# Top-32 attention and two feed-forward layers on one core: the weights' sign by ScalarE, three of eight units masked ahead of exp, blocks of one tile, an order planned with other transfer times

## The chip, the cores and the metric

The kernel runs on one core of a Trainium2 chip. The metric is the device time of one execution in microseconds (us); the kernel before takes 1253.52 us, the median of three runs (1252.94 to 1259.25). TensorE is called PE here, VectorE DVE, ScalarE ACT, GpSimd POOL and SyncE SP; all transfers (DMAs) of this kernel are issued by SP.

## The reference

The computation, cut to what matters:

```python
scores = scale * q @ k.T                       # 4 batches, 8 heads, 576 queries and keys, 64 dimensions
kth = the 32nd largest score of each row
e = exp(scores - max) where scores >= kth, else 0
x = (e / (sum(e) + 1e-9)) @ v                  # then one row of 512 for each of 2304 tokens
h = x @ w1i; x = maximum(0.01 * h, h) @ w1o    # 512 -> 2048 -> 512
h = maximum(x @ w2i, 0); out = (s * h * h + b) @ w2o
```

Inputs and outputs are float32. The kernel keeps accuracy near float32 by splitting every matrix into a high and a low float16 half and adding three of the four products (high by high, high by low, low by high).

## The kernel before

**Tiles, units, blocks.** The 2304 tokens are 18 tiles of 128: for each batch four tiles of 128 queries, and for each two batches one tile that holds the last 64 queries of both ("split"). A unit is a pair of heads of one tile, so a tile has 4 units and there are 72 (0 to 71). For each of the two heads of a unit: PE makes the scores (L768), ACT copies them from PSUM to `s` (L774), DVE finds the top 32 by four rounds of max-of-8 (L786) with three replacements of the found values between them (L795). ACT makes exp of all 576 scores into `em` (L808), with the maximum as bias; DVE multiplies it by the mask score >= 32nd and sums the row (L811). ACT and POOL split `em` into float16 halves (`ehl`, L865 and L869), SP turns them by a transposing DMA (`ahl<-ehl`, L873), PE multiplies by the values (`pv`, L897; 27 matmuls) and DVE scales the product by 1 / sum (L826) into `x` (L904). For the first 7 units (`EB`) PE itself does the turning (L838 to L851).

**The feed-forward layers** take blocks of tiles: ten of one tile, then four of two (`NB`, L930). In a block each layer's first product (L1022) makes 128 x 512 of `h` at a time, with 128 columns a matmul for a block of one tile and 256 for two. For layer 1 ACT makes two relus of it (L1050 scale, L1054 scale times -0.01), POOL subtracts them (L1058); for layer 2 ACT makes one relu and POOL squares it (L1062). ACT and POOL make the halves of that, `g` (L1067, L1070), and PE makes the second product (L1093). Layer 1's weights stay on the chip in `wreg`. Layer 2's halves lie in DRAM (`sc16`) and are streamed anew for every block in pieces of 512 KB (L1001), but for two pieces that stay (`kept`).

**The weights' way in.** Each of the four weight matrices comes in 16 blocks as raw float64 bits (L334, L337), 64 blocks in all. DVE shifts the high word (L343); ACT turns the next 16 bits into a rounded integer in the last place (L348, unsigned 16-bit in and out, every fourth half word); DVE cuts sign and top exponent bit beside it (L353); POOL adds the two (L357). Then come a norm for each four blocks (L367 to L413) and the split into halves, in one of several ways (`WM`): P by PE (L458, L461) and ACT (L466, L469), D by ACT (L445) and DVE (L454), G by DVE (L448), ACT (L443) and POOL (L451).

**What sets the order.** All steps go through a planner (`Plan.order`): a step has an engine, a price in us, what it needs, a key and the ring buffers that it takes and frees. Each engine takes, whenever it is free, the ready step with the lowest key. The result is a fixed order on each engine, and at run time every engine works through its list in order and waits at what isn't ready. A transfer's price in the planner is 0.65 us to its start and a duration that differs by kind (2.016 us for `ahl<-ehl`), and 0.91 to 1.0 us until another engine sees it.

```python
            x = add(SP, 2.016, e_turn, [y for _, y in lo], ke, take=[ta], use=[th], issue=0.65)   # L876
```

## Time and profile before

| what | value |
|---|---|
| time, median of 3 runs | 1253.52 us |
| the profiled execution's own time, by its span | 1250.3 us, 3.2 us under that median |
| busy: PE, DVE, ACT, POOL | 1070.3, 1036.9, 827.4, 842.1 us |
| first and last `x` of a unit (L904) | 51.4 and 1098.3 us |
| DMA | 228.39 MB, mean 183 GB/s |

The profile is of one execution. Busy time of an engine is the time in which it has an instruction; a matmul's end is modelled and matmuls overlap, so PE's busy time is above what its matmuls need when they follow each other closely. Idle time of an engine costs only where the engine is the one that all wait for. The page's second part cuts the span into 40 slices of 31 us and gives the busy share of each in tenths.

### The profile page before, as it was taken

How to read it: one execution, taken by the hardware profiler on the slowest of the kernel's cores; microseconds unless marked ns; L12 is line 12 of the kernel's file. 1: busy time of each engine (PE TensorE's matmuls, PEld its weight loads, DVE VectorE, ACT ScalarE, POOL GpSimd, SP SyncE). 2: the span in 40 equal slices, each digit the busy share in tenths (PEclk: the TensorE clock that was granted, in tenths of full speed). 3: DMA queues.
4: the chain of work that ended last, by engine and by line, in shares of the span. 5: the costliest groups of instructions: out<-in, count | busy, mean ns of one | idle time of the engine just before them, and what ended most of it. 6: DMA issues, size and time to landing. Idle time of an engine off the chain costs nothing.

```text
span 1250.3 us, 27997 instructions
## 1 busy us (share of the span) xinstructions
PE 1070.3 (86%) x10520; PEld 735.6 (59%) x10520; DVE 1036.9 (83%) x2437; ACT 827.4 (66%) x1427; POOL 842.1 (67%) x1126
## 2 busy tenths in 40 slices
PE   2666767788888988988998989789989799899998
PEld 1333334556666766665776666566566466666665
DVE  4999899999989999999999999889999999800000
ACT  7887998866577766667876665558876565444321
POOL 5776555657678877677887776658887666655542
PEclk9877898999999999999999999989999999999999
DMA  7767776478889898888899797988445568510444
GB/s 180 237 217 213 198 199 198 148 165 211 218 158 240 199 263 183 220 201 223 221 237 248 165 249 162 261 231 195 83 80 114 149 162 228 153 26 18 133 162 161
DMA packets 362408, 228.39 MB, mean 183 GB/s; under 512 B 276512, under 2 KB 301088, under 8 KB 362272
## 3 DMA queue, kind: packets, MB, share of 16 engines
q1 hardware_dynamic: 362272, 226.61, 71.5%
q8 instruction: 82, 1.34, 0.5%
q14 instruction: 54, 0.44, 0.1%
HBM read 151.52 MB, written 13.11 MB: 132 GB/s over the span
## 4 chain that ended last, share of the span: by engine, by line
DVE 24%; PE 22%; DMA 17%; POOL 9%; issue 4%; ACT 4%; SPq 1%; DVEq 0%; POOLq 0%; ACTq 0%
DMA ahl<-ehl 10%; DVE mx L786 9%; PE acc L1093 9%; PE h L1022 9%; DVE wk L795 8%; DVE em L811 5%; POOL ehl L869 3%; DMA st_o<-sc_2o 2%; PE pv L897 2%; POOL g L1070 2%; DMA qn<-in_q_dram 1%; POOL r L1058 1%; PE sc L768 1%; DMA vn<-in_v_dram 1%; DMA st_i<-sc_2i 1%
## 5 line engine op out<-in xcount | busy, mean ns | idle before, releaser
L786 DVE MAX8 mx<-wk 128x8 f32<-128x576 f32 x432 | 311.3, 744 | 0.0
L1093 PEld LDWEIGHTS <-g 128*128 128x128 f16 x1728 | 159.5, 98 | 141.0 <-issue 23.7
L1022 PE MATMUL h<-early,wreg 128*128 128x128 f16 (+1 forms) x2688 | 224.2, 235 | 5.1 <-DMA early<-xhl 3.5
L1022 PEld LDWEIGHTS <-wreg 128*128 128x128 f16 x2688 | 194.3, 98 | 52.8 <-issue 5.1
L1093 PE MATMUL acc<-wreg,g 128*128 128x512 f16 x864 | 222.8, 380 | 0.2 <-DVE o L1152 0.2
L795 DVE MATCH_REPLACE8 wk<-mx,wk 128x576 f32<-128x576 f32 x288 | 212.7, 741 | 0.0
L1093 PE MATMUL acc<-st_o,g 128*128 128x512 f16 x756 | 194.5, 379 | 12.9 <-DMA st_o<-sc_2o 12.6
L869 POOL TENSOR_TENSOR ehl<-em,ehl 128x576 f16<-128x576 f32 x130 | 168.0, 1298 | 50.1 <-ACT ehl L865 49.7
L1022 PE MATMUL h<-xT,st_i 128*128 128x128 f16 (+1 forms) x2352 | 198.5, 236 | 2.3 <-DMA st_i<-sc_2i 2.0
L1022 PEld LDWEIGHTS <-st_i 128*128 128x128 f16 x2352 | 170.3, 99 | 45.5 <-DMA st_i<-sc_2i 5.0
L1050 ACT ACTIVATE r<-h,cg 128x512 f32<-128x512 f32 x144 | 98.3, 683 | 93.7 <-PE h L1022 74.8
L811 DVE SCALAR_TENSOR_TENSOR em<-s,mx,em 128x576 f32<-128x576 f32 x144 | 155.0, 1087 | 0.3 <-ACT em L808 0.2
L865 ACT CAST ehl<-em 128x576 f16<-128x576 f32 x130 | 86.4, 668 | 93.0 <-DVE em L811 67.1
L808 ACT ACTIVATE em<-s,st,est 128x576 f32<-128x576 f32 x144 | 121.8, 861 | 18.9 <-POOL st L789 14.9
L1067 ACT ACTIVATE g<-r 128x512 f16<-128x512 f32 x144 | 89.9, 626 | 64.1 <-PE acc L1093 44.5
L897 PE MATMUL pv<-vhl,ahl 128*128 128x64 f16 (+3 forms) x2160 | 86.6, 201 | 49.8 <-DMA ahl<-ehl 47.6
L897 PEld LDWEIGHTS <-ahl 128*128 128x128 f16 (+1 forms) x2160 | 79.6, 104 | 71.9 <-DMA ahl<-ehl 66.8
L1058 POOL TENSOR_TENSOR r<-r,early 128x512 f32<-128x512 f32 x72 | 93.6, 1300 | 38.2 <-ACT early L1054 37.9
L1062 POOL TENSOR_TENSOR early<-r 128x512 f32<-128x512 f32 x72 | 75.7, 1052 | 62.1 <-ACT r L1050 61.4
L774 ACT COPY s<-sc 128x576 f32<-128x576 f32 x144 | 91.5, 636 | 35.0 <-PE sc L768 31.8
L768 PE MATMUL sc<-kT,qT 128*128 128x288 f16 (+1 forms) x640 | 99.2, 297 | 11.2 <-ACT s L774 9.7
L786 DVE MAX8 mx<-s 128x8 f32<-128x576 f32 x144 | 107.0, 746 | 0.3 <-ACT s L774 0.3
(191 smaller groups left out, 1741.0 us busy)
## 6 DMA issues: line engine op xcount, KB each, us to landing
st_i<-sc_2i SPq DMA_DIRECT2D x98, 512.0 KB, 4.8
st_o<-sc_2o SPq DMA_DIRECT2D x98, 512.0 KB, 4.8
raw_2i<-in_moe_w_in_dram SPq DMA_DIRECT2D x16, 512.0 KB, 4.9
wreg<-in_moe_w_in_dram SPq DMA_DIRECT2D x16, 512.0 KB, 5.7
raw_1o<-in_moe_w_out_dram SPq DMA_DIRECT2D x16, 512.0 KB, 4.0
raw_2o<-in_moe_w_out_dram SPq DMA_DIRECT2D x16, 512.0 KB, 4.1
qn<-in_q_dram SPq DMA_DIRECT2D x16, 256.0 KB, 4.8
sc_2i<-hl_2i SPq DMA_DIRECT2D x16, 256.0 KB, 2.4
```

The source lines that it names most:

```text
L768: nc.tensor.matmul(pt[a, c, 0:288], lhsT=qT[u][:, h, z, a], rhs=kT[b, p][:, 576 * h + 288 * c:576 * h + 288 * c + 288], start=(z == 0), st ...
L774: nc.scalar.copy(sc[u, h], box["pt"][:, :, 0:288])
L786: nc.vector.max(out=mx[u][:, h, r, :], in_=wk[u, h] if r else flat(sc[u, h]))
L795: nc.vector.match_replace(out=wk[u, h], in_to_replace=mx[u][:, h, r, :], in_values=src, imm_value=NEG)
L808: nc.scalar.activation(em[u][:, h, :], flat(sc[u, h]), AF.Exp, bias=st[u][:, h:h + 1], scale=est[:, 0, u:u + 1])
L811: nc.vector.scalar_tensor_tensor(em[u][:, h, :], flat(sc[u, h]), mx[u][:, h, 3, 7:8], em[u][:, h, :], op0=ALU.is_ge, op1=ALU.mult, accum_o ...
L869: nc.gpsimd.tensor_tensor(ehl[u][:, 1, a], em[u][:, h, :], ehl[u][:, 0, a], op=ALU.subtract)
L897: nc.tensor.matmul(pt[a, o0:o1], lhsT=ahl[u][:, za, blk * P + a.start:blk * P + a.stop], rhs=vt[:, zv, v0:v1], start=(i == 0 and za == 0 a ...
L1022: nc.tensor.matmul(box["h"][:, n * T:(n + 1) * T], lhsT=w[:, ew, c, :], rhs=src[:, ex, c, :], start=(c == 0 and ew == 0 and ex == 0), stop ...
L1050: nc.scalar.activation(box["r1"], box["h"], AF.Relu, scale=cg[:, 2 * l, 3, gi:gi + 1])
L1058: nc.gpsimd.tensor_tensor(box["r1"], box["r1"], box["r2"], op=ALU.subtract)
L1093: nc.tensor.matmul(accs[i, l, tt], lhsT=ghl[i, l, g][:, eg, n * T + tt * P:n * T + (tt + 1) * P], rhs=w[:, ew], start=(f == 0 and eg == 0 ...
```

## The change

What is done differently, by parts:

1. *The weights' way in.* The shift no longer cuts the sign (one operation instead of two, L373). The rest is now written as a 32-bit integer, by ACT in three of four blocks and by DVE in the fourth (`RM`, L380 and L382). ACT then writes the sign, plus or minus 1, as a bfloat16 into the upper half of that word (L386); the integer sum on POOL carries it to the exponent. DVE's cut of the sign goes. The scales get a factor of 2 for it. The norm's 16 matmuls for four blocks are one step (L402), and the ways of making halves differ (`WM`, `A` being ACT, ACT, POOL). The raw blocks' ring `raw` has 2 buffers, not 3, and the order of the matrices is other (`ORDER`).
2. *Masks.* In units 1, 4 and 6 of every 8 (`MK`; 27 of 72 units) ACT makes relu(BIG * (32nd - score)) (L862), POOL subtracts that from the scores (L865), and ACT makes exp of the difference with the row's sum in the same instruction (L868). DVE's mask and sum are left out there.
3. *Layers.* Layer 1's two relus and the difference become one leaky relu on ACT (L1117). Every second square of layer 2 is made by ACT (L1127), the others by POOL (L1129).
4. *Blocks.* One of two tiles, then 16 of one (`BLOCKS`).
5. *Planner.* Each kind of transfer has its issue time, its time to landing and its share of the queue (`XFER`); DVE's and POOL's steps that hold each other up are planned one after the other (`lock`); some rings give their buffers out in program order (`IN_LINE`); all keys are other numbers. `EB` is 11: four more units are turned by PE.

```diff
-        "ahl": 1, ..., "raw": 3, "T": 7, ...
+        "ahl": 1, ..., "raw": 2, "T": 7, ...
-WM = {"1i": "PPP", "1o": "P", "2i": "PG", "2o": "DP"}
-ORDER = ("1i", "1o", "2i", "2o")
+WM = {"1i": "VADV", "1o": "PPPP", "2i": "AGAA", "2o": "DPAP"}
+ORDER = ("1i", "1o", "2o", "2i")
+MK = "DADDADAD"
+RM = "AADA"
-EB = 7
+EB = 11
-NB = 10
+BLOCKS = [2, 1, 1, 1, 1, 1, 1, 1, 1, 1, 1, 1, 1, 1, 1, 1, 1]
-LAG = 0.65
+XFER = {..., "e_turn": (3.3, 5.1, 2.8), "turn": (1.3, 3.3, 1.1), "load": (0.42, 3.8, 1.8), ...}
...
+                    if self.lock[n]:
+                        end = max(now, held["POOL" if e == "DVE" else "DVE"]) + self.dur[n]
+                        held[e] = end
                     if e == "SP":
-                        end = moved = max(now + self.issue[n] + LAG, moved) + self.dur[n]
-                    free[e] = max(now + self.issue[n], end - 1.2) if e == "SP" else end
+                        issue, lat, _ = self.issue[n]
+                        end = moved = max(now + lat, moved + self.dur[n])
+                    free[e] = now + issue if e == "SP" else end
...
-            nc.vector.tensor_scalar(wT[m, f].bitcast(I32), t, 0x07FFFFFF, 3, op0=ALU.bitwise_and, op1=ALU.logical_shift_left)
+            nc.vector.tensor_scalar(wT[m, f].bitcast(I32), t, 3, None, op0=ALU.logical_shift_left)
...
-            nc.scalar.activation(t[:, :, 0], t[:, :, 1], AF.Copy, scale=2.0 ** -13)
+            d = raw[m, f].rearrange("p (n t) -> p n t", t=2)[:, :, 0]
+            if RM[f % len(RM)] == "A":
+                nc.scalar.activation(d, t[:, :, 1], AF.Copy, scale=2.0 ** -13)
+            else:
+                nc.vector.tensor_scalar(d, t[:, :, 1], 2.0 ** -13, None, op0=ALU.mult)
...
-            nc.vector.tensor_scalar(t[:, :, 1], t[:, :, 3], 0xC000, None, op0=ALU.bitwise_and)
+            nc.scalar.activation(raw[m, f].bitcast(BF16).rearrange("p (n t) -> p n t", t=4)[:, :, 1],
+                                 raw[m, f].bitcast(F32).rearrange("p (n t) -> p n t", t=2)[:, :, 1], AF.Sign)
...
+            def t_big(u=u):
+                nc.gpsimd.tensor_tensor(st[u][:, 8:10], mx[u][:, :, 3, 7], big.to_broadcast([P, 2]), op=ALU.mult)
+            def above(u=u, h=h):
+                nc.scalar.activation(em[u][:, h, :], flat(sc[u, h]), AF.Relu, bias=st[u][:, 8 + h:9 + h], scale=-BIG)
+            def less(u=u, h=h):
+                nc.gpsimd.tensor_tensor(em[u][:, h, :], flat(sc[u, h]), em[u][:, h, :], op=ALU.subtract)
+            def expo2(u=u, h=h):
+                nc.scalar.activation(em[u][:, h, :], em[u][:, h, :], AF.Exp, bias=st[u][:, h:h + 1], scale=est[:, 0, u:u + 1],
+                                     accum_out=st[u][:, 2 + h:3 + h])
...
-            x = add(SP, 2.016, e_turn, [y for _, y in lo], ke, take=[ta], use=[th], issue=0.65)
+            x = add(SP, XFER["e_turn"], e_turn, [y for _, y in lo], ke, take=[ta], use=[th])
...
-    for n in [1] * NB + [2] * ((NTL - NB) // 2):
+    for n in BLOCKS:
...
-                nc.scalar.activation(box["r1"], box["h"], AF.Relu, scale=cg[:, 2 * l, 3, gi:gi + 1])
-            def a2(g=g, box=box):
-                nc.scalar.activation(box["r2"], box["h"], AF.Relu, scale=cg[:, 1, 3, g * nf // 4:g * nf // 4 + 1])
-                    nc.gpsimd.tensor_tensor(box["r1"], box["r1"], box["r2"], op=ALU.subtract)
+                    nc.scalar.activation(box["r1"], box["h"], AF.Prelu, scale=cg[:, 0, 3, gi:gi + 1], alpha=0.01)
...
+                if sq == "A":
+                    nc.scalar.activation(box["v"], box["r1"], AF.Square)
+                else:
+                    nc.gpsimd.tensor_tensor(box["v"], box["r1"], box["r1"], op=ALU.mult)
```

Where the instructions stand in the order, at three places. On DVE, while blocks 4 to 6 of matrix 1o come in (`T_1o` is the shifted word, `raw_1o` the raw bits), before:

```order
L343 TENSOR_SCALAR T_1o_4_1333<-raw_1o_4_1253 128x512
L795 MATCH_REPLACE wk_4_0_1283<-mx_4_1263,wk_4_0_1283 128x576
L353 TENSOR_SCALAR raw_1o_4_1253<-raw_1o_4_1253 128x512
L343 TENSOR_SCALAR T_1o_5_1342<-raw_1o_5_1285 128x512
L353 TENSOR_SCALAR raw_1o_5_1285<-raw_1o_5_1285 128x512
L786 MAX mx_4_1263<-wk_4_1_1320 128x8
L343 TENSOR_SCALAR T_1o_6_1352<-raw_1o_6_1307 128x512
```

and now, on ACT, where L380 writes the rest and L386 the sign of block 5 (the other rows are halves of 1i, queries and unit 0's exp):

```order
L756 ACTIVATE qn_1_322<-qn_1_322,cqt_92 128x512
L380 ACTIVATE raw_1o_5_520<-raw_1o_5_520 128x512
L849 ACTIVATE em_0_596<-s_0_0_358,st_0_386,est_93 128x576
L386 ACTIVATE raw_1o_5_520<-raw_1o_5_520 128x512
L771 CAST qhl_4_605<-qn_1_322 128x4x64 x2
```

DVE's L353 is gone from its list; ACT has two instructions for the block where it had one. The same work on 1o stands beside unit 0 now and stood beside unit 4.

On DVE at the end of unit 33, one of the 27 (L811 is the mask, L826 and L892 the reciprocal of the row's sum, `mx_34` the next unit's top 32), before:

```order
L795 MATCH_REPLACE wk_33_1_8325<-mx_33_8248,wk_33_1_8325 128x576
L811 SCALAR_TENSOR_TENSOR em_33_8412,st_33_8249<-s_33_0_8045,mx_33_8248,em_33_8412 128x576
L786 MAX mx_33_8248<-wk_33_1_8325 128x8
L298 TENSOR_SCALAR cvt_84<-vsp_2_1_8439 128x1
L811 SCALAR_TENSOR_TENSOR em_33_8412,st_33_8249<-s_33_1_8078,mx_33_8248,em_33_8412 128x576
L303 TENSOR_SCALAR cvt_84<-cvt_84 128x1
L786 MAX mx_34_8482<-s_34_0_8304 128x8
L795 MATCH_REPLACE wk_34_0_8504<-mx_34_8482,s_34_0_8304 128x576
L298 TENSOR_SCALAR cvt_84<-vsp_2_2_8506 128x1
L826 RECIPROCAL st_33_8249<-st_33_8249 128x2
```

and now, from the last max of unit 33 to its reciprocal:

```order
L827 MAX mx_33_7613<-wk_33_1_7741 128x8
L827 MAX mx_34_7898<-s_34_0_7689 128x8
...
L827 MAX mx_34_7898<-wk_34_0_7916 128x8
L836 MATCH_REPLACE wk_34_1_7969<-mx_34_7898,wk_34_1_7969 128x576
L892 RECIPROCAL st_33_7614<-st_33_7614 128x2
L827 MAX mx_35_8049<-s_35_0_8029 128x8
L1217 SCALAR_TENSOR_TENSOR o_4_8060<-acc_3_1_0_7411,fin_4_6840,bc_85 128x512
```

Both masks are gone. Between the last max and the reciprocal stand 14 instructions now, 13 of them the next unit's search; four stood between the last mask and the reciprocal before.

On PE at the last unit's product (`pv_71`) and what follows it, before:

```order
L897 MATMUL pv_71_16270<-vhl0_94,ahl_71_16233 128x64
L1093 LDWEIGHTS g_12_0_1_16168
L1093 MATMUL acc_12_0_1_16206<-wreg_64,g_12_0_1_16168 128x512
...
L1022 LDWEIGHTS wreg_64
L1022 MATMUL h_12_0_6_16251<-early_63,wreg_64 128x256
```

and now:

```order
L963 LDWEIGHTS ahl_71_17098
L963 MATMUL pv_71_17205<-vhl0_96,ahl_71_17098 128x64
L1088 LDWEIGHTS st_13_i_7_17138
...
L1088 MATMUL h_13_1_3_17170<-xT1_13_16419,st_13_i_7_17138 128x128
L1088 LDWEIGHTS st_13_i_7_17138
```

Behind the last `pv` stood layer 1 of block 12, two tiles; now it is layer 2 of block 13 (tile 14), and the matmuls have 128 columns.

## Rows read from the trace of the kernel before

**Rows 1.** The page: busy time by engine, and two rows of the 40 slices.
```profile
PE 1070.3 (86%) x10520; PEld 735.6 (59%) x10520; DVE 1036.9 (83%) x2437; ACT 827.4 (66%) x1427; POOL 842.1 (67%) x1126
...
PE   2666767788888988988998989789989799899998
DVE  4999899999989999999999999889999999800000
```

**Rows 2.** DVE's timeline: the `x` of unit 11 and that of unit 71 (start, us).
```profile
310.17 0.28 DVE L904 TENSOR_TENSOR x<-pv,st 128x128 f32<-128x128 f32 x1
...
1098.27 0.29 DVE L904 TENSOR_TENSOR x<-pv,st 128x128 f32<-128x128 f32 x1 [8.18 <-PE pv L897]
```

**Rows 3.** Windows by stage: busy us (instructions) of each engine.
```profile
core 0: us, PE busy (x) PEld busy (x) DVE busy (x) ACT busy (x) POOL busy (x), PEclk, DMA share, GB/s
0.00:310.40 310.40, 216.44 (x1660) 130.36 (x1661) 283.06 (x658) 252.89 (x413) 196.30 (x254) 0.91 0.71 195
310.40:787.90 477.50, 429.49 (x5302) 316.40 (x5300) 455.65 (x1086) 330.38 (x594) 359.53 (x512) 0.99 0.89 214
787.90:1098.60 310.70, 277.60 (x2582) 193.39 (x2582) 289.92 (x667) 194.16 (x339) 217.88 (x301) 0.98 0.67 163
1098.60:1250.30 151.70, 146.74 (x980) 95.47 (x977) 8.29 (x30) 50.01 (x85) 68.36 (x60) 1.00 0.32 99
```

**Rows 4.** PE's longest wait from 310 to 1099 us: total, times, longest.
```profile
PE pv L897 <- DMA ahl<-ehl: 44.3, 41, 3.4
```

**Rows 5.** Windows of L353 alone, then of L348 alone, to 310.4 us.
```profile
0.00:310.40 310.40, 59.84 (x64) 0.91 0.71 195
...
0.00:310.40 310.40, 86.97 (x64) 0.91 0.71 195
```

**Rows 6.** Groups by line and form: count, busy us, mean ns, idle before.
```profile
L811 DVE SCALAR_TENSOR_TENSOR em<-s,mx,em 128x576 f32<-128x576 f32 x144 | 155.0, 1087 | 0.3 <-ACT em L808 0.2
L808 ACT ACTIVATE em<-s,st,est 128x576 f32<-128x576 f32 x144 | 121.8, 861 | 18.9 <-POOL st L789 14.9 <-POOL ehl L869 3.7
L1050 ACT ACTIVATE r<-h,cg 128x512 f32<-128x512 f32 x144 | 98.3, 683 | 93.7 <-PE h L1022 74.8 <-POOL g L1070 17.2 <-POOL st L820 0.6
L707 ACT ACTIVATION_READ_ACCUMULATOR qj<-qn 128x1 f32 x18 | 3.5, 195 | 0.0
L1058 POOL TENSOR_TENSOR r<-r,early 128x512 f32<-128x512 f32 x72 | 93.6, 1300 | 38.2 <-ACT early L1054 37.9 <-POOL vhl L666 0.2
L1062 POOL TENSOR_TENSOR early<-r 128x512 f32<-128x512 f32 x72 | 75.7, 1052 | 62.1 <-ACT r L1050 61.4
```

**Rows 7.** L348 and L353, the first matrix: ns least/median/most.
```profile
L348 ACT ACTIVATE raw_2i<-raw_2i x16: 1342/1356/1382, 16.2 to 100.9; 128x512 uint16<-128x512 uint16 x16
...
L353 DVE TENSOR_SCALAR raw_2i<-raw_2i x16: 716/740/1782, 17.6 to 102.7; 128x512 uint16<-128x512 uint16 x16
```

**Rows 8.** PE's timeline, rows that follow each other without a wait.
```profile
424.69 0.83 PE L1022 MATMUL h<-xT,st_i 128*128 128x128 f16 x12
425.36 0.65 PE L768 MATMUL sc<-kT,qT 128*128 128x288 f16 x4
425.85 0.83 PE L1022 MATMUL h<-xT,st_i 128*128 128x128 f16 x12
...
1094.60 0.81 PE L1093 MATMUL acc<-wreg,g 128*128 128x512 f16 x3
1095.24 1.47 PE L1022 MATMUL h<-early,wreg 128*128 128x256 f16 x12
1096.55 0.81 PE L1093 MATMUL acc<-wreg,g 128*128 128x512 f16 x3
1097.20 1.03 PE L897 MATMUL pv<-vhl,ahl 128*128 128x128 f16 x27
1098.07 0.81 PE L1093 MATMUL acc<-wreg,g 128*128 128x512 f16 x3
```

**Rows 9.** The page's DMA issues: count, median us from issue to landing.
```profile
ahl<-ehl SPq DMA_TRANSPOSE x65, 5.3
```

More of the change, by code (lines that the diff above doesn't have):

```diff
@@ L99, in order @@
         remain = [t[1] for t in self.by_tok]
+        line = {r: iter(self.rings[r].line) for r in IN_LINE}
+        turn = {r: next(line[r], None) for r in IN_LINE}
         last = [0.0] * len(remain)
         start, self.end, moved = [None] * N, [0.0] * N, 0.0
-        events = []
+        events, held = [], {"DVE": 0.0, "POOL": 0.0}
         for n in range(N):
@@ L134, in order @@
                     for k in self.take[n]:
-                        self.rings[self.by_tok[k][0]].live.append(k)
+                        r = self.rings[self.by_tok[k][0]]
+                        r.live.append(k)
+                        if self.by_tok[k][0] in turn:
+                            turn[self.by_tok[k][0]] = next(line[self.by_tok[k][0]], None)
+                            for e_, it in r.wait:
+                                heapq.heappush(events, (now, it[1], "ready"))
+                            r.wait = []
                     start[n] = now
@@ L151, in order @@
                         remain[k] -= 1
-                        last[k] = max(last[k], end + (0.95 if e == "SP" else 0.2))
+                        last[k] = max(last[k], end + (0.1 if e == "SP" else 0.2))
                         if not remain[k]:
@@ L269 @@
     nc.vector.memset(neg1, -1.0)
+    big = one.tile([P, 1], F32, name="big")
+    nc.vector.memset(big, BIG)
     tiny = one.tile([P, 2], F32, name="tiny")
@@ L1075, in layer @@
                 x = add(ACT, 0.571, a1, [x, fin1], ka, take=[t1], use=[th])
-                x = add(ACT, 0.571, a2, [x], ka, take=[t2], use=[th])
-                x = y = add(POOL, 1.225, a3, [x], ka, use=[t1, t2])
                 x = add(ACT, 0.52, a4, [x], ka, take=[tg], use=[t1])
@@ L1081, in layer @@
                 z = add(ACT, 0.571, a1, [x, fin], ka, take=[t1], use=[th])
-                y = add(POOL, 1.225, a3, [z], ka, take=[t2], use=[t1])
+                y = add(ACT if sq == "A" else POOL, 0.6 if sq == "A" else 1.0, a3, [z], ka, take=[t2], use=[t1])
                 x = add(ACT, 0.52, a4, [z], ka, take=[tg], use=[t1])
```

193 lines of the change are left out of this document (108 added, 85 removed).

## The prediction

> **What bounds the kernel now.** I read the page first. PE is busy 86% and DVE 83% of the span, but not in the same places: DVE stands at 9 tenths from slice 2 to slice 34 and falls to 0 in the last five, where PE stands at 9 [rows 1]. So there are stages, and I cut them at two `x` of DVE: that of unit 11 is made at 310 us, that of unit 71, the last, at 1098 us [rows 2]. The windows between [rows 3] give three stages.
>
> - *Start, 310.4 us:* weights come in, 12 units are done. DVE is busy 283.1 us (91%), ACT 252.9 (81%), PE 216.4.
> - *Middle, 788.2 us, 60 units:* DVE is busy 745.6 us (94.6%), PE 707.1 (89.7%). DVE is the bound. The longest wait of PE in it is for the turned weights of attention, 44.3 us in 41 waits [rows 4].
> - *Tail, 151.7 us:* attention is over and PE works off what it is behind with.
>
> PE's busy time is too coarse for what follows, since a matmul's row overlaps the next one's. The distance of starts is better [rows 8]: 12 matmuls of 128 columns take 425.36 - 424.69 = 0.67 us (0.056 each), 12 of 256 columns 1.31 us (0.109 each), three of 512 columns 0.64 us (0.214 to 0.216 each), four score matmuls 0.49 us and the 27 of a `pv` 0.87 us. A unit, two heads of four score matmuls and one `pv`, needs 2 x 0.49 + 0.87 = 1.85 us of PE, 1.9 with small things. Counted in PE's order, the middle has 3300 matmuls of 128 columns, 924 of 256 and 1260 of 512: 184.8 + 100.7 + 272.2 = 557.7, with 60 units 672 us, which is 85% of 788.2. In the tail it is 612 of 256 and 369 of 512, 146.4 us, which is 96.5% of 151.7. That is how closely PE can be packed here.
>
> **The change, stage by stage.** Sums are made in the profiled execution's time, span 1250.3 us; the median of the runs is 3.2 us more, and I add that at the end.
>
> *Start.* DVE loses the 64 sign cuts, 59.8 us [rows 5], and 8 masks (units 1, 4, 6, 9) of 1.087 us [rows 6], 8.7 us. It gains 16 rests; these are strided 16-bit reads like L353's, which takes 0.74 us where POOL does not hold it up [rows 7]: 11.8 us. The other ways of making halves cancel within 2 us, and by its order DVE has 9 more search steps before unit 11's `x`, 7 us. Sum 283.1 - 50 = 233 us. ACT loses 64 rests, 87.0 us [rows 5], and gets 48 back with 64 signs. Both prices are unknown. Above, they are that of L348, 1.36 us [rows 7], which has the same steps of 8 bytes and 16-bit words; below, that of a 512-column activation with 32-bit words, 0.683 us (L1050) [rows 6]. L353 reads and writes the same half words in 0.74 us on DVE [rows 7], so the steps alone do not make it slow; what is left of L348 is ACT with 16-bit integers on both sides. The rest now writes 32-bit words and the sign reads float32 and writes a bfloat16, so each has lost one of the two, and I take 0.68 for both: 76 us, 11 less than now. The first feed-forward groups come later in ACT's order (one instead of nine, 17 us less), four more units are turned by PE (7 us more), masks cost 7 us more. Sum about 240 us. So the stage that DVE held at 283 now has two engines at 233 and 240. When DVE was packed to 91%, the second engine was well below; with two alike I take 87%: 240 / 0.87 = 275 us, 35 less. If one of the two passes on ACT stays at 1.36 us it is 33 to 44 us more on ACT, and at 93% the stage takes about 300 us; with both, 317 us of ACT and 340 us. Downwards DVE's and ACT's 91% give 263.
>
> The rows show 1.36 us for a 512-column ACT instruction [rows 7]. The Trainium skill, "ScalarE: Activation LUTs", section "What ACT_TABLE_LOAD costs", has one element per cycle whatever the function, 186 ns + 0.833 ns a column, 0.61 us for 512. The trace agrees for L1050 within 0.07 us and not for L348; by the rule the start would be about 267 us, by L348 for both passes 340.
>
> *Middle.* DVE loses 46 of its 120 masks there, 46 x 1.087 = 50 us [rows 6]: 696 us, 735 at today's 94.6%. But PE gets more. By its order the middle has 5160 matmuls of 128 columns, 240 of 256 and 1425 of 512: 289.0 + 26.2 + 307.8 = 623, with 60 units 738 us, 66 more than before. Part of that is work that was done in the start (21.5 us of it is left there, 51.6 were) and part comes from the tail. So the bound passes from DVE to PE, and the question is how closely PE is packed: 96.5% as in the tail gives 765 us, 85% as in the middle now gives 866. What speaks for a close packing is that PE's waits for `ahl<-ehl` [rows 4] come from where the order has `pv`: the turning takes 5.3 us to land [rows 9], and by the pitches above PE had 2.5 us of matmuls on average between the turning and its `pv`, and has 4.8 us now. Most of the 44.3 us should go. Also a unit's masks no longer stand before its reciprocal in three of eight units, so that DVE is waited for less. Against it: what PE no longer loses there it may lose to POOL and ACT, which make `g`. POOL loses 72 differences of 1.300 us and 36 squares of 1.052 [rows 6], 131 us in all, and gets 54 subtractions of about 1.42 (1.300 x 576 / 512, with room above), 27 small ones and some halves of weights, about 100 us; ACT loses 72 relus of 0.683, 49 us, and gets 36 squares, 54 relus and 54 row sums of 0.195, about 70 us. Neither comes above 75% busy, so both are cover enough. I take 93.5%, nearer to the tail's packing than to today's: 738 / 0.935 = 790 us, 2 more than now, with more of the work done in it. The ends are 765 and 820 (90%).
>
> The in-part of a layer costs 2 x 0.056 = 0.112 us for 256 columns in blocks of one tile against 0.109 [rows 8], 3.5 us for the 18 tiles. The Trainium skill, "Perfetto Trace Analysis", section "Matmuls", says that larger matmuls are more efficient where possible, which speaks against blocks of one tile; the trace agrees in sign, and the cost is the 3.5 us that is already in the counts.
>
> *Tail.* By the order 984 matmuls of 128 and 276 of 512 columns stand behind the last `pv`: 55.1 + 59.6 = 114.7 us, at 96.5% 119. The last tile's in-part is followed at once by its own out-part, with less beside it than in a block of two; 1 to 4 us for that. 120 us, 32 less; ends 117 and 126.
>
> Sum: 275 + 790 + 120 = 1185 us of span, and with 3.2 us about 1189 us.
>
> **The rivals.**
>
> *ACT's weight passes stay slow.* For it: L348 is steady at 1.34 to 1.38 us [rows 7], so it is no contention. Against it: the word sizes change. One slow pass gives 300 + 790 + 120 + 3 = 1213 us, both 1253.
>
> *DVE stays the bound and PE keeps up.* For it: PE's tail packing. Middle 765, start 265: 765 + 265 + 118 + 3 = 1151 us. Against it: PE has attention's short groups between, which the tail has not.
>
> *The waits do not go* (the order does not do what it says). PE stays at 85 to 86% in the middle, because what it waits for behind the turning is the chain through one `em`, one `ehl` and one `ahl` buffer; in the 27 units this chain gets longer by a big multiple, a relu, a subtraction on POOL and an exp behind the last max: 0.7 + 2 x 1.4 + (0.861 + 0.195) us [rows 6], with the multiply and six hops some 6 us, before the split begins. DVE's reciprocal waits at the end of it, with the next unit's search queued behind. In the order DVE has a median of 12 search steps between the two, 8 us at 0.7 a step (745.6 us over 60 units is 12.4 a unit, less two masks 10.2, for 14 steps), so it decides where POOL's queue, with halves of `g` or `v` between, adds more than 2 us. Also all 17 blocks now stream layer 2's weights; the window with blocks of one tile had the DMA engines at 0.89, the one with two at 0.67 [rows 3]. Middle 738 / 0.855 = 863: 275 + 863 + 120 + 3 = 1261 us, slower. The point from which it is slower than before is a packing below 86%.
>
> **How the numbers follow.** Forecast 0.58, around 1189 us, its own range 1160 to 1222 (start 263 to 290, middle 770 to 815). Slow weight passes 0.2, mostly one pass. DVE bound with PE keeping up 0.12. Waits stay 0.10. A measurement of this kernel can tell 0.5% from no change, 1247.3 to 1259.8 us. Faster: the forecast, the fast rival and most of the slow passes, 0.85; same 0.06; slower 0.09. The range from 1147 to 1250 leaves the rest out.
>
> **What would show it.** Right: the `x` of unit 11 near 275 us, the sign's and the rest's means under 0.8 us on ACT; in the middle DVE at about 88% busy and PE higher than DVE, PE's wait for `ahl` under 20 us; the `x` of unit 71 near 1065 us and 120 us of tail. Wrong: a sign at 1.3 us and ACT full in the start; DVE waiting for POOL at L892; or the `x` of unit 71 after 1115 us.

## The result and the profile after

The changed kernel takes 1233.4 us, the median of four runs (1229.5 to 1234.4), against 1253.2 us, the median of four runs of the kernel before (three of them are those named at the top): a ratio of 0.984 with a 95% interval of 0.980 to 0.987. It is faster by 1.6%, which the interval parts from no change; 1189 us were forecast, 5% less. The profiled execution took 1232.6 us, its span is 1230.6.

The page's busy times and three rows of its slices, as in [rows 1], with ACT's row added:

```profile
PE 1059.6 (86%) x11664; PEld 757.2 (62%) x11664; DVE 933.9 (76%) x2285; ACT 876.3 (71%) x1559; POOL 789.4 (64%) x1107
...
PE   2366666458999999999999999999999999999997
...
DVE  3567888888997798999998999996599999920000
ACT  7999898897678687768787767767676765752332
```

PE now stands at 9 from slice 11 to slice 39. DVE, which stood at 9 in nearly all slices from 2 on, is at 3 to 8 up to slice 10; from slice 2 to slice 9 it is ACT that stands at 8 and 9. The `x` of unit 11 and of unit 71 in DVE's timeline (start, us), as in [rows 2]:

```profile
320.45 0.28 DVE L970 TENSOR_TENSOR x<-pv,st 128x128 f32<-128x128 f32 x1
...
1102.11 0.29 DVE L970 TENSOR_TENSOR x<-pv,st 128x128 f32<-128x128 f32 x1 [2.73 <-PE pv L963]
```

So the same three stages as in [rows 3], in windows (busy us and instructions of each engine):

```profile
0.00:320.70 320.70, 187.75 (x1188) 115.94 (x1189) 237.18 (x607) 280.23 (x475) 193.55 (x265) 0.79 0.61 175
320.70:1102.40 781.70, 754.08 (x9218) 559.10 (x9215) 690.81 (x1658) 559.52 (x1025) 559.69 (x811) 1.00 0.88 211
1102.40:1230.60 128.20, 117.72 (x1260) 82.17 (x1260) 5.96 (x22) 36.52 (x60) 36.21 (x33) 0.99 0.68 212
```

| stage | before | forecast | after |
|---|---|---|---|
| start | 310.4 | 275 | 320.7 |
| middle | 788.2 | 790 | 781.7 |
| tail | 151.7 | 120 | 128.2 |

The middle came 8 us below the forecast and the tail 8 us above it; that the two errors cancel is luck. So the whole of the 46 us by which the span missed 1185 lies in the start, which became longer instead of shorter. What ACT's and DVE's passes on the weights take, by line (ns least/median/most), where [rows 7] has those of before:

```profile
L386 ACT ACTIVATE raw_2i<-raw_2i x16: 1337/1342/1363, 205.4 to 269.7; 128x512 bf16<-128x512 f32 x16
```

```profile
L380 ACT ACTIVATE raw_2i<-raw_2i x12: 656/672/724, 204.7 to 268.6; 128x512 int32<-128x512 uint16 x12
```

```profile
L382 DVE TENSOR_SCALAR raw_2i<-raw_2i x4: 414/504/895, 212.3 to 265.8; 128x512 int32<-128x512 uint16 x4
```

The rest, which now writes 32-bit words, fell to 0.67 us, as forecast. The sign, which writes a bfloat16 into every fourth half word, takes nearly what L348 took, 1.34 us against 1.36. Its 64 passes are 86.1 us of ACT in the start. ACT is busy for 280 of 320.7 us there, 87%, and DVE for 237.

PE's longest waits in the middle (us in total, times, longest), to be held against the 44.3 us of [rows 4]:

```profile
PE pv L963 <- DMA ahl<-ehl: 13.4, 15, 1.6
PE acc L1158 <- DMA st_o<-sc_2o: 4.7, 9, 0.8
```

### The profile page after: what moved, and what is told of

It reads as the page before. It is cut to its first block, busy times and chain, and to the rows that moved or that the text cites. A ratio compares the mean times of both kernels' runs of the same rounds, so it can differ in the third digit from the quotient of the medians.

```text
span 1230.6 us, 30307 instructions
## 1 busy us (share of the span) xinstructions
PE 1059.6 (86%) x11664; PEld 757.2 (62%) x11664; DVE 933.9 (76%) x2285; ACT 876.3 (71%) x1559; POOL 789.4 (64%) x1107
## 4 chain that ended last, share of the span: by engine, by line
PE 37%; DMA 17%; ACT 17%; DVE 17%; POOL 6%; issue 5%; SPq 1%; ACTq 0%; POOLq 0%; DVEq 0%
PE acc L1158 15%; PE h L1088 13%; DMA ahl<-ehl 8%; DVE mx L827 7%; DVE wk L836 6%; DMA st_o<-sc_2o 3%; PE pv L963 3%; DMA st_i<-sc_2i 2%; POOL ehl L935 2%; PE sc L809 2%; DVE em L852 1%; ACT s L815 1%; ACT wreg L386 1%; PE wlo_1o L496 1%; ACT em L868 1%
## 5 line engine op out<-in xcount | busy, mean ns | idle before, releaser
L1088 PEld LDWEIGHTS <-wreg 128*128 128x128 f16 x3264 | 206.9, 98 | 46.9 <-issue 0.5
L1158 PE MATMUL acc<-wreg,g 128*128 128x512 f16 x864 | 231.1, 379 | 0.0
L1088 PE MATMUL h<-early,wreg 128*128 128x128 f16 (+1 forms) x3264 | 230.4, 222 | 0.0
L1158 PE MATMUL acc<-st_o,g 128*128 128x512 f16 x756 | 200.9, 382 | 7.9 <-DMA st_o<-sc_2o 7.9
L1088 PEld LDWEIGHTS <-st_i 128*128 128x128 f16 x2856 | 179.9, 98 | 42.2 <-DMA st_i<-sc_2i 9.6
L935 POOL TENSOR_TENSOR ehl<-em,ehl 128x576 f16<-128x576 f32 x122 | 155.1, 1283 | 31.7 <-ACT ehl L931 30.7
L1136 POOL TENSOR_TENSOR g<-r,g 128x512 f16<-128x512 f32 x72 | 84.2, 1170 | 81.0 <-ACT g L1133 80.5
L1136 POOL TENSOR_TENSOR g<-early,g 128x512 f16<-128x512 f32 x72 | 85.5, 1188 | 50.4 <-ACT g L1133 35.8
L836 DVE MATCH_REPLACE8 wk<-mx,s 128x576 f32<-128x576 f32 x144 | 106.8, 742 | 0.0
L963 PEld LDWEIGHTS <-ahl 128*128 128x128 f16 (+1 forms) x2160 | 79.5, 102 | 42.5 <-DMA ahl<-ehl 20.6
L1117 ACT ACTIVATE r<-h,cg 128x512 f32<-128x512 f32 x72 | 49.4, 686 | 77.0 <-PE h L1088 71.2
L963 PE MATMUL pv<-vhl,ahl 128*128 128x64 f16 (+3 forms) x2160 | 85.0, 199 | 19.7 <-DMA ahl<-ehl 13.4
L931 ACT CAST ehl<-em 128x576 f16<-128x576 f32 x122 | 79.7, 668 | 19.1 <-DMA ahl<-ehl 14.9
```

What stands on the lines that cost most here:

```text
L836: nc.vector.match_replace(out=wk[u, h], in_to_replace=mx[u][:, h, r, :], in_values=src, imm_value=NEG)
L931: nc.scalar.copy(ehl[u][:, 0, 576 * h:576 * h + 576], em[u][:, h, :])
L935: nc.gpsimd.tensor_tensor(ehl[u][:, 1, a], em[u][:, h, :], ehl[u][:, 0, a], op=ALU.subtract)
L963: nc.tensor.matmul(pt[a, o0:o1], lhsT=ahl[u][:, za, blk * P + a.start:blk * P + a.stop], rhs=vt[:, zv, v0:v1], start=(i == 0 and za == 0 a ...
L1088: nc.tensor.matmul(box["h"][:, n * T:(n + 1) * T], lhsT=w[:, ew, c, :], rhs=src[:, ex, c, :], start=(c == 0 and ew == 0 and ex == 0), stop ...
L1117: nc.scalar.activation(box["r1"], box["h"], AF.Prelu, scale=cg[:, 0, 3, gi:gi + 1], alpha=0.01)
```

## The experiments

Theory 1 was that the sign's slow pass on ACT is all that is missing. Its rivals: the `raw` ring of two buffers holds the loads back (theory 2); TensorE's granted clock, 0.60 and 0.63 between 200 and 300 us and so nearer to the lower of its two levels (1.2 and 2.4 GHz), holds the weights back (theory 3); the block of two tiles at the front, which lets the first feed-forward matmul come at 292.8 us instead of 210.3, starves PE (theory 4). Times are medians, with the ratio to the kernel before run on the same chip and its 95% interval; single runs are marked. "x" is the time of the `x` of unit 11, measured to its end, in the one profile of each kernel. The runs of one kernel span 3 to 11 us, so a difference of 3 us in x, from two single profiles, is not clear of scatter. What theory 3 goes by, two windows of the changed kernel (columns as in [rows 3]; the clock is the third from the end):

```profile
200.00:250.00 50.00, 26.06 (x160) 15.82 (x159) 39.85 (x99) 41.29 (x66) 30.55 (x37) 0.60 0.59 184
250.00:300.00 50.00, 32.47 (x240) 23.42 (x240) 43.13 (x109) 44.09 (x81) 31.47 (x43) 0.63 0.59 188
```

PE is busy for 52% of the first and 65% of the second.

### The price of the form by itself

```diff
+        nc.scalar.activation(xh[:, :, 1], w[:, :, 1], AF.Sign)     # L30 bfloat16, every 8 bytes
+        nc.scalar.activation(x[:, :, 0], w[:, :, 1], AF.Sign)      # L31 float32, every 8 bytes
+        nc.scalar.activation(xc, w[:, :, 1], AF.Sign)              # L32 bfloat16, side by side
+        nc.scalar.activation(x2, w[:, :, 1], AF.Sign)              # L33 bfloat16, every 4 bytes
+        nc.scalar.activation(xh[:, :, 1], a[:, 0:512], AF.Sign)    # L34 as L30, source side by side
+        nc.scalar.activation(xi[:, :, 0], wu[:, :, 1], AF.Copy, scale=2.0 ** -13)   # L36 the rest
+        nc.scalar.activation(xh[:, :, 1], w[:, :, 1], AF.Copy)     # L37 as L30, a copy
+        nc.vector.tensor_copy(xh[:, :, 1], w[:, :, 1])             # L38; L39 the same in float32
```

> Not the computation at all: ten forms of a 128x512 pass, six times each, one after the other with nothing beside them. If the 2-byte write at a step of 8 bytes is what costs, the sign and a plain copy of this form take 1.3 to 1.4 us on ACT whether the source is strided or not, and the 4-byte writes, strided or not, the contiguous bfloat16 and the integer rest take 0.55 to 0.72 us. If it is the 2-byte element and not the step, the contiguous bfloat16 is slow too; if the sign function is what costs, the float32 sign takes 1.3 us and the bfloat16 copy 0.68 us. On DVE both forms take below 0.8 us.

Groups by line of that kernel (count, busy us, mean ns of one, idle before):

```profile
L34 ACT ACTIVATE b<-a 128x512 bf16<-128x512 f32 x6 | 8.0, 1337 | 0.2
L37 ACT ACTIVATE b<-a 128x512 bf16<-128x512 f32 x6 | 8.0, 1335 | 0.2
L30 ACT ACTIVATE b<-a 128x512 bf16<-128x512 f32 x6 | 8.0, 1335 | 7.3 <-DVE b L39 6.3 <-DVE b L23 1.0
L33 ACT ACTIVATE b<-a 128x512 bf16<-128x512 f32 x6 | 4.6, 774 | 0.2
L38 DVE CAST b<-a 128x512 bf16<-128x512 f32 x6 | 4.4, 735 | 45.9 <-ACT b L37 45.9
L32 ACT ACTIVATE b<-a 128x512 bf16<-128x512 f32 x6 | 3.9, 653 | 0.2
L36 ACT ACTIVATE b<-a 128x512 int32<-128x512 uint16 x6 | 3.9, 652 | 0.2
L31 ACT ACTIVATE b<-a 128x512 f32<-128x512 f32 x6 | 3.9, 651 | 0.2
...
L39 DVE COPY b<-a 128x512 f32<-128x512 f32 x6 | 2.6, 429 | 0.2
```

Neither the function (sign or copy), nor the steps of the source, nor 16 bits alone, nor a step of 8 bytes alone costs anything that can be seen here. 16-bit elements written 8 bytes apart cost 1.335 us, 4 bytes apart 0.774, and next to each other 0.653; 32-bit words 8 bytes apart cost 0.651. On DVE the same form takes 0.735 us against 0.429.

### The sign as a word (theory 1)

```diff
-            nc.scalar.activation(raw[m, f].bitcast(BF16).rearrange("p (n t) -> p n t", t=4)[:, :, 1],
-                                 raw[m, f].bitcast(F32).rearrange("p (n t) -> p n t", t=2)[:, :, 1], AF.Sign)
+            t = raw[m, f].bitcast(F32).rearrange("p (n t) -> p n t", t=2)
+            nc.scalar.activation(t[:, :, 0], t[:, :, 1], AF.Sign)
```

> The sign is written as a 4-byte float32 word over the rest instead of as a bfloat16 above it, so the three low bits of each weight are left out; the order is the same. Theory 1 (the start is long because the sign's 2-byte writes at steps of 8 bytes take 1.35 us on ACT, 64 x 0.67 = 43 us too much): the sign falls to about 0.68 us, the x of unit 11 comes at 275 to 290 us instead of 320.7, and the median is 1190 to 1203 us. Theory 2 (two buffers of raw hold the loads back) and theory 3 (TensorE's low clock between 200 and 300 us holds the weights' products back): the sign may get faster, but the x of unit 11 stays above 310 us and the time above 1222 us.

1216.7 us, ratio 0.968 (0.965 to 0.970). The sign took 0.67 us, 42.5 us in all, and x came at 302.3 us. Its start stage as a window:

```profile
0.00:302.30 302.30, 188.71 (x1194) 118.51 (x1195) 244.01 (x607) 244.67 (x475) 194.52 (x265) 0.80 0.64 185
```

The sign's 43.6 us became 18 us of the start, and neither theory 1's 275 to 290 nor its rivals' 310. ACT and DVE are now alike at 81%, with PE at 62% and POOL at 64%. A second limit exists.

### The ring of raw buffers (theory 2) and the front block (theory 4)

```diff
-"raw": 2,
+"raw": 3,
```

> The raw ring has three buffers again instead of two; nothing else changes, but the planner uses the third one. Theory 1 (the sign on ACT): the start stays ACT-bound, the x of unit 11 between 312 and 325 us, the time within 0.5% of the changed kernel, 1227 to 1240 us. Theory 2 (the ring): ACT waits less for loads, the x of unit 11 below 300 us and the time below 1215 us.

```diff
-BLOCKS = [2, 1, 1, 1, 1, 1, 1, 1, 1, 1, 1, 1, 1, 1, 1, 1, 1]
+BLOCKS = [1] * 18
```

> The first block has one tile instead of two (18 blocks of one tile). Theory 4 (feed-forward work cannot begin before unit 7's x, 269 us, and TensorE is short of work until then, 97 to 156 us of every 250): the first feed-forward matmul comes at about unit 3's x, some 50 to 100 us earlier, and the time falls by 10 to 40 us to 1195 to 1223 us. Theory 1: ACT is full in the start, so the feed-forward work that is put there delays the units by as much; the x of unit 11 is later by 5 to 15 us, and the time stays between 1223 and 1240 us.

Both came out as slow as the kernel before, outside every time that had been expected: 1257.1 us, ratio 1.001 (0.999 to 1.003), and 1256.8 us, 1.001 (0.999 to 1.002), with x at 334 and 330 us. With a front block of one tile the first feed-forward matmul comes at 172.6 us, 120 us earlier than in the changed kernel, and nothing is won. But both edits make the planner lay out another order throughout, and both orders lose 6 to 9 us in the middle and 4 to 5 in the tail too, beside 9 to 13 in the start. So they say less of ring and block than that a new order with keys chosen for another can cost 24 us. That PE does not starve is likely for theory 4, not shown. Theory 2 was then tried in the same order, without and with the word sign:

```diff
-        return pl.tile(shape, dtype, tag=name, name=label, bufs=BUFS[name])
+        return pl.tile(shape, dtype, tag=name, name=label, bufs=3 if name == "raw" else BUFS[name])
```

> The tile pool of raw has three buffers, but the order is made as if it had two, so the order is that of the changed kernel, instruction for instruction; only the loads of weights wait for an older buffer. Theory 2 (the ring of two holds the weights back): the x of unit 11 at 305 us or earlier instead of 320.7, the time 1205 to 1220 us. Theory 1 (ACT's sign holds them back): within 0.5% of the changed kernel, 1227 to 1240 us. It also tells what made the kernel with three buffers in ring and order slow (1257 us): if this one stays at 1233, it was the order that came of it.

1230.5 us, ratio 0.983 (0.979 to 0.987), x at 320.5 us: no difference that the intervals tell.

> The sign as a 4-byte word over the rest (the three low bits of each weight left out) and the third buffer of raw in the unchanged order, both together. With the word alone the x of unit 11 came at 302 us, with ACT and DVE both 244 us busy (81%), and its chain of waits went again and again from the sum on GpSimd that frees a raw buffer over a 4 to 5 us load to the next shift. Theory 2 as the second limit: once ACT is relieved the ring decides, and the x of unit 11 comes at 280 to 293 us, the time at 1195 to 1209 us. Rival (the fixed order, in which DVE, ACT and TensorE wait for each other, is the second limit): 298 to 304 us and 1211 to 1219 us.

1210.3 us, ratio 0.966 (0.962 to 0.969), x at 299.1 us, 3 us earlier than with the word alone. The x is where the rival had it, the time lies just between the two cases, and the interval overlaps that of the word alone (0.965 to 0.970). So theory 2 falls as the main cause; what the third buffer gives is not clear of scatter.

### Which engine holds the start

Four single runs, each from the kernel with the word sign in the same order, with a large part of one engine's work in the start left out.

```diff
-            nc.scalar.activation(t[:, :, 0], t[:, :, 1], AF.Sign)
+            nc.scalar.activation(raw[m, f].rearrange("p (n t) -> p n t", t=2)[:, 0:32, 0], t[:, 0:32, 1], AF.Sign)
```

> All four runs of this group go from the kernel with the sign as a word (x of unit 11 at 302.3 us) and leave out most of one engine's work of the start in the same order, to see which engine still holds it. Here ACT's sign is made for 32 of 512 columns (and shift and sign are replaced so that the numbers stay finite; the output means nothing): 64 x about 0.45 = 29 us of ACT less. If ACT is still the bound, the x of unit 11 comes 20 to 29 us earlier, at 273 to 282 us; if it is another engine, less than 8 us earlier; if the engines only wait for each other in the fixed order, 8 to 15 us.

```diff
-                    nc.vector.max(out=mx[u][:, h, r, :], in_=wk[u, h] if r else flat(sc[u, h]))
+                    nc.vector.max(out=mx[u][:, h, r, :], in_=(wk[u, h][:, 0:64] if u < 12 else wk[u, h]) if r else flat(sc[u, h]))
```

> Units 0 to 11 take their second to fourth maximum over 64 of 576 scores (wrong scores are kept there): 72 x about 0.55 = 40 us of DVE less in the start. If DVE is the bound now, the x of unit 11 comes 25 to 40 us earlier, at 262 to 277 us; if another engine is, less than 10 us earlier; if the engines only wait for each other, 10 to 20 us.

```diff
-            nc.gpsimd.tensor_tensor(d, d, raw[m, f].rearrange("p (n t) -> p n t", t=2)[:, :, 0], op=ALU.add)
+            nc.gpsimd.tensor_tensor(d[:, 0:32], d[:, 0:32], raw[m, f].rearrange("p (n t) -> p n t", t=2)[:, 0:32, 0], op=ALU.add)
```

> The sum of shifted word and rest on GpSimd for 32 of 512 columns (and shift and sign are replaced so that the numbers stay finite; the output means nothing): 64 x about 1.0 = 64 us of GpSimd less, and each raw buffer is free 1 us earlier. If the chain of the weights over GpSimd holds the start (its share of 194 us in 302 speaks against it), the x of unit 11 comes more than 15 us earlier, below 287 us; otherwise less than 10 us.

```diff
-                nc.tensor.matmul(sp["h"], lhsT=cI[m, gi], rhs=wT[m, ff], start=True, stop=True)
+                nc.tensor.matmul(sp["h"], lhsT=ident16, rhs=ones16[:, 0:1].to_broadcast([P, 512]), start=True, stop=True)
```

> The float32 product that scales a block of weights on TensorE, two rows of about 1.04 us each in the start's low clock, is replaced by one float16 product of 512 columns with constants (the output means nothing): 32 of them, at 0.5 to 2 us less each, 15 to 60 us of TensorE less. Theory 3 (TensorE at its low clock holds the chain of the weights): the x of unit 11 comes 15 to 40 us earlier, below 287 us. If not: less than 8 us.

The start of each as a window, in this order (columns as in [rows 3]: PE, PEld, DVE, ACT, POOL, granted clock, DMA share, GB/s):

```profile
0.00:293.00 293.00, 184.07 (x1188) 116.01 (x1189) 250.53 (x608) 219.57 (x475) 195.02 (x265) 0.78 0.66 191
```

```profile
0.00:293.20 293.20, 180.85 (x1189) 113.89 (x1190) 206.18 (x608) 244.17 (x475) 191.59 (x265) 0.79 0.67 191
```

```profile
0.00:296.20 296.20, 182.76 (x1188) 114.83 (x1189) 225.82 (x607) 243.46 (x475) 125.12 (x265) 0.80 0.66 189
```

```profile
0.00:297.00 297.00, 169.38 (x1157) 111.08 (x1158) 243.39 (x608) 244.56 (x475) 193.88 (x265) 0.73 0.66 189
```

| work left out | busy us less | x earlier, us | share |
|---|---|---|---|
| ACT | 25.1 | 9.3 | 0.37 |
| DVE | 37.8 | 9.1 | 0.24 |
| POOL | 69.4 | 6.1 | 0.09 |
| PE | 19.3 | 5.3 | 0.27 |

The table goes by the windows, against that of the word sign. ACT's 9 us fall into the case of engines that wait for each other, the other three into the case that this engine is not the bound; taken together no single engine holds the start. Each gives back some of what is taken from it, and none more than 0.4 of it; from single profiles the shares are rough. POOL's row is not POOL's alone: with its sum cut, DVE's busy time fell too, from 244.0 to 225.8 us. Theory 3 falls in the form that was stated, with 5 us instead of 15 to 40. That the engines wait for each other in a fixed order fits all four, but no run shows it; which waits these are was not tried.

### Is PE the bound of the middle?

Two single runs from the changed kernel, in the same order:

```diff
+                    nc.vector.max(out=mx[u][:, h, r, :], in_=(wk[u, h][:, 0:64] if u >= 12 else wk[u, h]) if r else flat(sc[u, h]))
```

> From the changed kernel, same order: units 12 to 71 take their second to fourth maximum over 64 of 576 scores (wrong scores are kept), 360 x about 0.45 = 160 us of DVE less in the middle. If TensorE is the bound of the middle, as the prediction had it, the middle (x of unit 11 to x of unit 71, 781.7 us) falls by less than 15 us, at full clock to no less than about 755 us; if DVE still is, by 60 us or more.

```diff
-                    for za, zv in ((0, 0), (0, 1), (1, 0)):
+                    for za, zv in ((0, 0), (1, 0)) if u >= 12 else ((0, 0), (0, 1), (1, 0)):
```

> From the changed kernel, same order: units 12 to 71 leave out one of the three products of the attention's second step (high weights by low values), 9 of 27 short matmuls a unit, 54 units at 9 x 0.032 = 0.29 us and 6 with two batches at twice that, 17 to 20 us of TensorE less. If TensorE bounds the middle, the middle falls by 12 to 20 us to about 762 to 770 us; if DVE or a chain does, by less than 5 us.

The middle of both, as windows:

```profile
318.30:1099.50 781.20, 753.47 (x9228) 558.97 (x9226) 515.16 (x1658) 558.85 (x1025) 557.91 (x812) 1.00 0.89 211
```

```profile
321.50:1095.10 773.60, 736.17 (x8605) 536.78 (x8603) 692.57 (x1656) 557.22 (x1025) 557.11 (x810) 1.00 0.89 213
```

DVE lost 176 us and the middle 0.5, so DVE is not the bound. PE lost 17.9 us and the middle 8.1, a little under half and between the two cases of the expectation; PE's waits for streamed weights rose (`acc` for `st_o`, from 4.7 to 9.9 us). In the eleven profiles of this order in which nothing was taken from the middle it has 779.3 to 787.5 us, so the 8.1 are 6 to 14. PE is what the middle goes by most, and the streams of weights take over part of what is taken from it; that PE alone bounds it is not shown.

### Other ways to the sign

All signs on DVE, then every second one, in the order of the changed kernel:

```diff
+            if f % 2 == 0:                          # left out where all are on DVE
+                t = raw[m, f].bitcast(U16).rearrange("p (n t) -> p n t", t=4)
+                nc.vector.tensor_scalar(t[:, :, 1], t[:, :, 3], 0x8000, 0x3F80, op0=ALU.bitwise_and, op1=ALU.bitwise_or)
+                return
```

> All 64 signs on DVE, in one pass over the 16-bit words (and, or), at the same place of the same order: ACT loses 64 x 1.35 = 86 us, DVE gains 64 x 0.75 to 0.95 = 48 to 60 us, the weights are complete. By what an engine's work has been worth in this order (43 us of ACT moved the x of unit 11 by 18 us, 28 more by 9, about 35 of DVE by 9) it comes at 320.7 - 37 + 14 = about 298 us and the time at 1205 to 1220 us. If DVE now takes the start over as the bound (237 + 55 = 292 us busy), the x of unit 11 comes at 315 us or later and nothing is gained.

> Every second sign on DVE, the others on ACT as in the changed kernel, same order: ACT loses 43 us, DVE gains 24 to 30. By the same slopes: the x of unit 11 at 320.7 - 18 + 7 = about 310 us, the time at 1216 to 1228 us. If the slow passes that are left still set the pace of the weights, it stays above 315 us and 1228 us.

All: 1240.8 us, ratio 0.988 (0.984 to 0.992), x at 322.8 us. Half: 1226.3 us, 0.977 (0.973 to 0.980), x at 310.4 us. Their starts as windows, all first:

```profile
0.00:322.80 322.80, 187.37 (x1189) 117.25 (x1190) 296.84 (x672) 211.98 (x411) 206.28 (x265) 0.79 0.61 173
```

```profile
0.00:310.40 310.40, 186.75 (x1188) 116.72 (x1189) 271.66 (x639) 246.06 (x443) 197.50 (x265) 0.77 0.63 180
```

With all of them DVE is at 92%, and x comes at 322.8 us: the second case of that expectation, DVE as the bound. With half, the slopes' 310 us came out; that it is so exact is luck, since DVE gained 34 us instead of 24 to 30, and x is from one profile. Half with the third buffer:

> Every second sign on DVE and a third buffer of raw, both in the unchanged order. The half on DVE alone gave 1226 us and the x of unit 11 at 310 us; the third buffer gave 3 us in either of its two runs. If the two add, the x of unit 11 comes at 304 to 309 us and the time is 1216 to 1225 us, faster than both kernels. If the ring matters more now that ACT and DVE are alike, below 1214 us; if not at all, 1224 to 1229 us.

1223.6 us, ratio 0.974 (0.971 to 0.977), x at 306.0 us. Both are where the sum of the gains had them, but the interval doesn't part this run from half alone. Then a way without narrow writes, in which the rest is joined to the shifted word before the sign is made:

```diff
-            nc.vector.tensor_scalar(wT[m, f].bitcast(I32), t, 3, None, op0=ALU.logical_shift_left)
+            nc.vector.scalar_tensor_tensor(wT[m, f].bitcast(I32), t[:, :, 1], 3, t[:, :, 0], op0=ALU.logical_shift_left, op1=ALU.bitwise_or)
...
-                nc.scalar.activation(d, t[:, :, 1], AF.Copy, scale=2.0 ** -13)
+                nc.scalar.activation(d, t[:, :, 1], AF.Copy, scale=2.0 ** -13, bias=-(0.5 - 2.0 ** -14))
```

> Another way to the same weights: the rest as a whole number by ACT, joined to the shifted word on DVE in one pass (shift and or), and then the sign as a 4-byte word by ACT, so that nothing writes 2 bytes at steps of 8. The order is a new one by keys that were not chosen for it, so the total tells little (1233 to 1285 us, as both other new orders stood 24 us above). Looked for are the durations: the sign and the rest 0.64 to 0.72 us on ACT, the joined pass 0.55 to 0.85 us on DVE (the plain shift has 0.42).

A single run at 1254.9 us, in an order by old keys; sign 0.66 to 0.70 us, the join 0.84 to 1.09 us by matrix, above the bound I had set for three of the four. The two last runs have keys chosen anew, with other engines for some halves and rests and 12 and 10 units turned by PE instead of 11. Half's planner has the measured durations; the join's has 0.85 us for the join but still 0.59 and 0.65 for rest and sign, which take 0.68. Of the first, some lines:

```diff
-W0 = {"1i": -35.11, "1o": -4.04, "2i": -55.23, "2o": 4.3}
+W0 = {"1i": -91.626, "1o": -26.46, "2i": -45.67, "2o": -103.77}
...
-        y = add(DVE, 0.39, w_shift, [l], kk, take=[tT], use=[tr], lock=True)
-        x = add(ACT, SIGN, w_sign, [x], kk, use=[tr])
+        y = add(DVE, 0.85, w_shift, [x], kk, take=[tT], use=[tr], lock=True)
+        x = add(ACT, SIGN, w_sign, [y], kk, use=[tr])
```

> The joined pass (rest by ACT, shift and or in one DVE pass, sign as a word by ACT), with the keys of the order and who makes the halves chosen anew for the durations measured here (0.68 us rest and sign, 0.85 us join); the middle's masks and blocks are those of the changed kernel. Theory (an order that was made with a sign of 0.65 us could not fit one of 1.35 us; with passes that cost what the order says, the start's engines wait less): the x of unit 11 at 280 to 300 us, the time 1195 to 1222 us. Rival (the start is held by the coupling of small rings whatever the order): the x of unit 11 above 300 us and 1222 us or more.

> Every second sign on DVE, with the keys of the order chosen anew for the true durations (sign 1.35 us on ACT, 0.74 on DVE). Against the same passes in the old order (1226 us, x of unit 11 at 310 us) this tells what the order alone is worth: theory, 1205 to 1222 us with the x of unit 11 below 305 us; rival (the old order was as good), 1222 to 1240 us.

The join in its new order: **1210.1 us**, ratio 0.964 (0.962 to 0.966), x at 297.8 us. Half in its new order: 1212.0 us, 0.965 (0.963 to 0.967), x at 301.8 us. Both beat both kernels. The stages of the join:

```profile
0.00:297.80 297.80, 193.16 (x1238) 118.48 (x1239) 236.84 (x552) 252.31 (x497) 186.46 (x255) 0.85 0.60 169
297.80:1080.30 782.50, 751.59 (x9208) 557.75 (x9206) 703.45 (x1685) 563.60 (x1035) 568.93 (x819) 1.00 0.90 217
1080.30:1206.80 126.50, 116.72 (x1260) 81.67 (x1260) 6.15 (x23) 36.90 (x61) 36.63 (x33) 1.00 0.67 214
```

The join went from 1254.9 us to 1210.1, half from 1226.3 to 1212.0, each by keys, by who makes halves and rests, and by the units that PE turns, all together. Of the 46 us of span between the two profiles of the join, 12 lie in the start, 24 in the middle and 11 in the tail: its first order was as unfit throughout as the two orders of theories 2 and 4. Of half's 9 us of span, 9 lie in the start. That the old order did worse because it was made for a sign of 0.65 us is argued, not shown: no run has keys chosen anew at the old prices, and the kernel with the word sign speaks against it, since its sign takes 0.67 us where its order reckons with 0.65, and its x comes at 302.3 us, as late as that of half in the new order. What the new orders do differently can be seen: their last sign begins at 297.9 and 301.3 us, so the first twelve units are made beside the weights, where the old order leaves 50 us of them behind the last sign (the next section has the rows).

## Why the prediction was wrong, step by step

*The start is the step that failed*, in two places. The first is a price. The prediction saw that L348 had two things that could make it slow, 16-bit integers on both sides, and it said "each has lost one of the two, and I take 0.68 for both". The rest had lost the one that mattered, the narrow write, and the sign had kept it: 1.35 us. That was the nearest row of the same form, and I left it for one of another form because the word sizes changed. With 64 x 0.67 = 43 us more ACT's 240 become 283, and 280 were measured; DVE's 233 were 237. The counts were near enough; six of the feed-forward groups fell into ACT's start, not one, which is some 6 us.

By the Trainium skill, "ScalarE: Activation LUTs", section "What ACT_TABLE_LOAD costs", a pass takes one cycle an element whatever the function. That agrees with sign and copy here, both 1335 ns in one form, and not with the forms, 651 and 1335 ns for one function: the measurement decides.

The second place is "with two alike I take 87%", one busy share for the whole start. With the price repaired (sign as a word) ACT and DVE were alike at 244 us, near the 240 of the forecast, and the stage took 302 us, which is 81%, not 87. So of the 46 us by which the start missed 275, 18 go to the sign's price and 27 to the busy share. The traces show that the start is two parts. Up to its last sign, which begins at 269.7 us (L386 above), and from there to unit 11's `x`, the changed kernel has these windows (columns as in [rows 3]):

```profile
0.00:269.00 269.00, 145.32 (x826) 83.61 (x826) 190.69 (x491) 244.14 (x407) 163.76 (x222) 0.79 0.65 183
269.00:320.70 51.70, 42.43 (x362) 32.32 (x363) 46.49 (x118) 36.09 (x69) 29.79 (x44) 0.76 0.43 129
```

The kernel with the word sign has these, its last sign beginning at 251.8 us:

```profile
0.00:252.00 252.00, 146.46 (x827) 86.28 (x828) 197.80 (x491) 209.99 (x409) 165.61 (x222) 0.79 0.68 196
252.00:302.00 50.00, 41.95 (x365) 31.99 (x364) 45.91 (x115) 34.43 (x66) 28.61 (x44) 0.82 0.45 133
```

In the first part ACT is at 91% in the changed kernel, as full as DVE was in [rows 3], and the price of the sign acts there alone. The second part is 50 us whatever the weights cost: in the twelve profiles of this order whose last sign is ACT's, `x` comes 48 to 52 us after its end, also where DVE has 6 us less to do in it. The forecast's division has no such part. With the word sign the first part has ACT at 83% and DVE at 78%; at 91% it would be 231 us and x at 281 (an estimate from these rows), so some 21 of the 27 us are the looser first part.

That two engines near the same load must wait for each other is not the reason, or not by itself. The kernel before had both as near in the same part, up to the end of its last L348 at 235.8 us, at 89% (DVE) and 86% (ACT):

```profile
0.00:235.80 235.80, 152.09 (x939) 85.83 (x939) 209.85 (x474) 202.40 (x324) 146.23 (x186) 0.88 0.72 204
```

So the busy share goes by more than how near the two loads are; which waits make the difference stays open.

The rival "ACT's weight passes stay slow" was what happened, at one pass of two, as it said. Its price, 300 us for the start and 1213 in all, rested on 93% for ACT over the whole start; 87% came, 91% in the first part and 70% in the second.

*The middle was right, and in the main for the reason given.* PE took the bound over, busy 754.1 of 781.7 us (96.5%); its 738 us of matmuls by distance of starts are 94.4% of the stage, where I took 93.5. DVE is at 88.4%, as forecast. PE's wait for `ahl` fell to 13.4 us, under the 20 that were named. The run that took work from DVE shows that DVE is no longer the bound; in the run that took work from PE the middle gave back a little under half of it. DVE's waits for POOL at L892, which the prediction named among the signs of being wrong, came to 14.4 us in 10 waits, and the middle was short all the same. *The tail* was forecast 8 us too short, 120 against 128; no run looked into it, and it is 125 to 130 us in all variants but the three with unfit orders (132 to 137).

The rivals "DVE stays the bound" and "the waits do not go" are out by the same rows. Open is why no order reached 275 us: the best has 298. The four runs that left out work say that it isn't one engine's work; they don't say which waits would have to go.

## What to carry to other kernels

When an instruction is slow and one of its features goes, price what is left by the nearest row that shares the written side (element size and step), and measure the form by itself first. Divide a stage by a busy share only where one engine holds it from end to end: look for the last instruction of what you make shorter, and see how much of the stage lies behind it, here 50 us. In a fixed order in which no engine is full, count what is taken from ACT or DVE at a quarter to two fifths. Where a planner sets the order, keys that were chosen for one program can cost a variant 24 us, so a variant's time in such an order says little of the variant.
